# A gated mix of two attentions: the keys' first half loaded behind the first queries, and the first unit's maxima taken half by half

## The chip, the cores and the metric

The kernel runs on one core of one Trainium2 chip. The metric is the device time of one execution in microseconds; of several runs the median is given.

## The reference

Two attention blocks read the same input `x` (2048 rows, 448 columns, 16 heads of 28) and are mixed row by row by a sigmoid gate.

```python
qkv = x @ wqkv                       # for A and for B, split into q, k, v of 16 heads
# A: each position sees itself and 7 earlier ones at a distance of 2
logits = einsum("bhsd,bhswd->bhsw", q, k[idx]) * 28 ** -0.5     # idx = pos - 2 * (0..7), masked
a = (softmax(logits) applied to v[idx]) @ A_wo
# B: full attention
p = softmax(einsum("bhqd,bhkd->bhqk", q, k) * 28 ** -0.5)
b = einsum("bhqk,bhkd->bhqd", p, v) @ B_wo
g = sigmoid((x * gate_w).sum(-1, keepdims=True))
out = g * a + (1 - g) * b
```

## The kernel before

The kernel's order is written out by hand: each engine takes its instructions in the order in which the program gives them. Nearly all DMAs are issued by one queue, SP (SyncE), also in program order. An instruction that waits holds up all that stand behind it on its engine, and a DMA whose source isn't ready holds up SP.

**Projection stage** (the first 250 us or so). The loop `for n, t in enumerate(tiles)` computes one tile of the product `x @ wqkv` a turn. The tiles 0 to 27 are B's queries and keys, 128 rows of the transposed product by 512 positions, then follow B's values and A's queries, keys and values. Each float32 operand is split in a rounded part and a rest (`hi`, `lo`; `xh`/`xl`, `wh`/`wl`), so a tile takes 11 matmuls. The order of the first tiles is, as (position block `nb`, row group `k`): (0,1), (0,0), (0,2), (1,1), (1,2), (1,0), (2,1), (3,1), (2,0), (2,2), (3,0), (3,2). Row group 1 holds the keys of the first four heads, row group 0 their queries. So the keys of positions 0 to 1023 come from tiles 0 and 3, those of 1024 to 2047 from tiles 6 and 7, and the first 512 queries from tile 1.

- The tiles 0 to 9 (`n < FULL`) use the whole array. `qk_tile` (L344 to L349) takes the result out of PSUM with ScalarE (L348) and VectorE (L349), and `qk_store` sends both parts to DRAM (`qk_hi`, `qk_lo`) on SP, through `dma_r` (L99).
- From tile 10 on `project_halves` works with the two 64-row halves of the array side by side: 21 half matmuls a tile. ScalarE copies both partial sums (L353, `raw`), GpSimd adds them (L355), ScalarE rounds (L358) and GpSimd takes the rest (L359). The copy and the `hi`/`lo` pair lie in a pool of eight rotating buffers (`pp`, `pair`).

**The maxima, spread over the program.** B's softmax needs each query's maximum over all keys ahead of its exponentials. For that the scores are computed a first time with the rounded parts. A unit `u` is 512 queries of four heads; there are 16. A unit's maxima are 64 matmuls of 128 queries (`qs`) by 512 keys (`kc`) for one head (`h`), issued by `s1_mm` (L142), and VectorE reduces each result to one number per query (L148, L164) in a column of `MX`. From tile 11 on each tile of the projection carries four of these matmuls (`s1_half`), which stand behind the second and the eighth of the tile's products in each half. A unit thus spans 16 tiles. In the first unit the number `i` of a matmul within the unit gives `qs = i // 16`, `kc = i // 4 % 4`, `h = i % 4`: tile 11 reads keys 0 to 511, tile 12 keys 512 to 1023, tile 13 keys 1024 to 1535, tile 14 keys 1536 to 2047, all for the first 128 queries, and so on.

When a unit's 64 maxima are there, `max_parts` folds the four of each query and head with one reduction on VectorE (L176), and ScalarE and GpSimd turn the result into two parts, which go to DRAM (`nm`) and are read with the queries of the attention stage.

**The loads for it.** `load_qhi(u)` brings a unit's queries to `QP` (four DMAs, one for each head, L99), and `load_k` brings keys to `KH` (four DMAs as well). In the loop the first queries are loaded at `n == 3`; the keys of the first four heads come in two halves, positions 0 to 1023 at `n == 5` and 1024 to 2047 at `n == 8`. In the same turns stand, in this order: the tile's own stores, the loads of the next weights (`load_w`, at `n` 2 and 3), `load_qhi(0)` and `load_k`.

**Attention stage** (from some 255 us). For each unit and each block of 128 keys TensorE computes the scores with three products (L980), ScalarE the exponentials (L985), TensorE their product with the values (L946); the rest of the maxima (L142, L148) and all of A's windowed attention (GpSimd, VectorE) are laid beside it by a planner with estimated costs. The last stage is the output projection (L832).

Of the kernel before, what the change touches and what calls it, by code (L numbers as in the profile page):

```python
# [11 lines left out]
ALU = mybir.AluOpType  # L12
X = mybir.AxisListType.X
ET = mybir.EngineType

S, D, H, DH = 2048, 448, 16, 28
# [5 lines left out]
NMX = 192  # L22
# [3 lines left out]
def gated_mix_kernel(ctx: ExitStack, tc: tile.TileContext, xT, xn, gw, wA, wB, woAB, out):  # L26
# [4 lines left out]
    qk_hi = dram.tile([2 * D, S], F32R, name="qk_hi")  # L31
# [39 lines left out]
    KH = [cp.tile([128, S], F32R, name=f"KH{i}") for i in range(2)]  # L71
    KL = [cp.tile([128, S], F32R, name="KL0")]
    MX = cp.tile([128, NMX], F32, name="MX")
# [24 lines left out]
    def dma_r(dst, src):  # L98
        nc.sync.dma_start(dst.bitcast(F32), src.bitcast(F32))  # L99


    def load_k(g, t, src, c=slice(0, S)):
        for h in range(4):
            r = D + 112 * g + DH * h
            dma_r(t[32 * h:32 * h + DH, c], src[r:r + DH, c])
# [23 lines left out]
    def load_qhi(u):  # L129
        g, b = divmod(u, NB)  # L130
        qhis[u] = QP[u % 2]
        for h in range(4):
            r = 112 * g + DH * h
            dma_r(qhis[u][h % 2][32 * h:32 * h + DH, :], qk_hi[r:r + DH, 512 * b:512 * b + 512])

    def s1_mm(n, bank, half=False):
        u, i = divmod(n, 64)
        qs, kc, h = i // 16, i // 4 % 4, i % 4
        if i == 0 and u + 1 < NU:
            load_qhi(u + 1)  # L140
        r = slice(64 * (h // 2), 64 * (h // 2) + 64) if half else slice(32 * h, 32 * h + DH)
        nc.tensor.matmul(bank, qhis[u][h % 2][r, 128 * qs:128 * qs + 128],  # L142
                         KH[u // NB % 3][r, 512 * kc:512 * kc + 512], start=True, stop=True)
# [29 lines left out]

    def max_parts(u, later=None):
        m = sp.tile([128, 16], F32, name="m")
        nc.vector.tensor_reduce(m.rearrange("p (h q) -> p q h", h=4),  # L176
                                MX[:, 64 * u % NMX:64 * u % NMX + 64].rearrange("p (q k h) -> p q h k", q=4, h=4),
                                axis=X, op=ALU.max)
        t = sp.tile([128, 32], F32R, name="nmt")
        v = sp.tile([128, 16], F32, name="nmv")  # L180
        nc.scalar.activation(t[:, 0:16], m, AF.Copy, scale=-1.0)
        nc.scalar.activation(v, m, AF.Copy, scale=-1.0)
        low = lambda: nc.gpsimd.tensor_tensor(out=t[:, 16:32], in0=v, in1=t[:, 0:16].bitcast(F32), op=ALU.subtract)
        if later:
            later(low)
        else:
            low()
        return t
# [6 lines left out]
    def max_store(u, r):  # L195
        for a in range(4):
            nc.sync.dma_start(nm[u].bitcast(F32)[:, 32 * a:32 * a + 32], r[32 * a:32 * a + 32, :])  # L197
# [14 lines left out]
    with tc.tile_pool(name="xp", bufs=1) as xp, tc.tile_pool(name="wp", bufs=2) as wp:  # L212
# [28 lines left out]
        def split_x(nb):  # L241
            r, t = xst[:, nb, 0:3, :], xst[:, nb, 3, :]
            for kt in range(3):
                split(xh[nb][:, kt, :], xl[nb][:, kt, :], r[:, kt, :])
            tail = xh[nb][:, 3, :]
            nc.scalar.activation(tail, t, AF.Copy)
            o = LOW[nb]
            nc.vector.tensor_tensor(out=tail[o], in0=t[o], in1=tail[o].bitcast(F32), op=ALU.subtract)
# [3 lines left out]
        def load_w(wi, tails=(False, True)):  # L252
            src, cols = WSRC[wi]
            if wi not in wraw:
                wraw[wi] = raw3(), wp.tile([128, 450], F32, tag="wt", name="wt"), sum(c1 - c0 for c0, c1 in cols) + 2 * (wi == GATE)
            r, t, _ = wraw[wi]
            for tail in tails:
                o = 0
                for c0, c1 in cols:
                    e = o + c1 - c0  # L260
                    if tail:
                        both(t[:, o:e], src[384:448, c0:c1])
                    else:
                        nc.sync.dma_start(r[:, :, o:e], src[0:384, c0:c1].rearrange("(k p) c -> p k c", p=128))
                    o = e

                if wi == GATE:
                    if tail:
                        both(t[:, o:o + 2], gw[0:2, 384:448].rearrange("i p -> p i"))
                    else:  # L270
                        for kt in range(3):
                            nc.sync.dma_start(r[:, kt, o:o + 2],
                                              gw[0:2, 128 * kt:128 * kt + 128].rearrange("i p -> p i"))

        def split_w(wi, kts):
            if wi not in wsets:
                wsets[wi] = [wp.tile([128, 4, 450], F32R, tag=g, name=f"{g}{wi}") for g in ("wh", "wl")]
            wh, wl = wsets[wi]
            r, t, n = wraw[wi]
            for kt in kts:  # L280
                split(wh[:, kt, :n], wl[:, kt, :n], r[:, kt, :n] if kt < 3 else t[:, :n], nc.gpsimd)
# [24 lines left out]
        def project(n):  # L306
            order = FIRST if n == 0 else ORDER
            for i, p in enumerate(order):
                product(n, p, None, i == 0, i == len(order) - 1)
                if n == 0 and i == 0:  # L310
                    warm(3)
# [109 lines left out]
        for kt in range(3):  # L421
            if kt < 2:
                nc.vector.tensor_copy(xh[0][:, kt, :], r[:, kt, :])
            nc.vector.tensor_tensor(out=xl[0][:, kt, :], in0=r[:, kt, :], in1=xh[0][:, kt, :].bitcast(F32),
                                    op=ALU.subtract)
        nc.vector.tensor_tensor(out=tail[64:128], in0=t[64:128], in1=tail[64:128].bitcast(F32), op=ALU.subtract)
        nc.vector.tensor_tensor(out=wl0[:, 3, 0:256], in0=wt0[:, 0:256], in1=wh0[:, 3, 0:256].bitcast(F32),
                                op=ALU.subtract)
# [3 lines left out]
        def split_third():  # L432
            c = slice(256, 384)
            for kt in range(3):
                split(wh0[:, kt, c], wl0[:, kt, c], wr1[:, kt, 128:256])
            split(wh0[:, 3, c], wl0[:, 3, c], wt0[:, c])
# [19 lines left out]
        for n, t in enumerate(tiles):  # L456
            wi = t[0]
            for w in loads:
                if loads[w] == n:
                    load_w(w)  # L460
            for w in splits:
                i, k = (n - splits[w][0]) * splits[w][1], splits[w][1]
                if 0 <= i < 4:
                    split_w(w, range(i, i + k))
            if n == 0:
                split_third()
            if n in (3, 5):
                split_x((n + 1) // 2)
            if n < FULL:
                project(n)  # L470
            else:
                project_halves(n, [S1_START <= m < S1_START + 80 for m in (n, n + 1)])
            if t[1] == "qk":
                qk_tile(n, t[2], t[3])
            elif t[1] == "v":
                add_halves(n, V[:, t[2], :, 0:DH])
            else:
                a_tile(n, t[2], t[3])
            if n == 0:
                split_x(1)  # L480
            while fini and fini[0][0] <= n:
                fini.pop(0)[1]()
            if n in (2, 3):
                load_w(1, (n == 3,))
            if n == 3:
                load_qhi(0)
            if n in (5, 8):
                load_k(0, KH[0], qk_hi, slice(0, 1024) if n == 5 else slice(1024, S))
            if n == 16:
                for i in (1, 2):  # L490
                    nc.sync.dma_start(a_scr[i][:, 0:NJ, :].rearrange("c j e -> c (j e)").rearrange(
                        "c (a b) -> c a b", b=NJ), omg[0:8, None, :].to_broadcast([8, 56, NJ]))
            if n == 32:
                nc.gpsimd.memset(V[:, :, :, DH:], 1.0)
            if n == 22:
                load_k(1, KH[1], qk_hi)
            if n == 62:
                load_k(0, KL[0], qk_lo)
            if parts and parts[0][0] <= n:
                _, u, t = parts.pop(0)  # L500
                max_store(u, max_turn(t))
            if finished and n < len(tiles) - 3:
                u = finished.pop(0)
                parts.append((n + 3, u, max_parts(u)))
            if n == 64:
                gate = []
                for sgn, dst in ((-1.0, g_t), (1.0, omg)):
                    e = sp.tile([128, NJ], F32, name="ez")
                    nc.scalar.activation(e, zt, AF.Exp, scale=sgn)
                    nc.gpsimd.tensor_tensor(out=e, in0=e, in1=V[:, 0, :, DH], op=ALU.add)  # L510
                    gate.append((dst, e))
            if n in (66, 68):
                nc.vector.reciprocal(*gate.pop(0))
            if n == 70:
                nc.sync.dma_start(og_scr.rearrange("(j p) -> p j", j=NJ), omg)
            if n == 76:
                load_q(0)
# [183 lines left out]
    for c in range(8):  # L701
# [20 lines left out]
        n = 0  # L722
# [321 lines left out]
    u = NU - 1  # L1044
# [30 lines left out]
```

## Time and profile before

| | |
|---|---|
| three timed runs | 904.98, 905.28, 903.61 us; median 904.98 |
| the profiled execution | 903.91 us, of which the span is 902.1 |
| granted TensorE clock, mean | 1.0 |
| TensorE matmuls | 8326, busy 895.1 us |
| VectorE, ScalarE, GpSimd busy | 737.1, 644.3, 640.5 us |
| DMA | 105.04 MB, mean 116 GB/s |

Times of instructions are counted from the start of the span. "PE" is TensorE's matmuls, "PEld" its weight loads, which run beside the matmuls before them; "SPq" is SP's queue, whose rows give the time of issuing a DMA and not that of its transfer. A row of the timeline gives start, duration, engine, line, operation, the tile written and the tiles read, the shape and the count; in brackets stands the idle time ahead of it with what ended it. A row of the waits gives a total, a count and the longest, in us. A row of the windows gives for a stretch the busy time of PE, PEld, DVE, ACT and POOL with their instruction counts, then the granted clock, the DMA engines' busy share and GB/s.

### The profile page before, as it was taken

Reading aid. Unit: us, or ns where it says so; the run is one execution under the profiler, and the core shown is the slowest. Engines: PE = TensorE matmul, PEld = TensorE weight load, DVE = VectorE, ACT = ScalarE, POOL = GpSimd, SP = SyncE. Lnnn points to the kernel's source line nnn. Section 1 sums busy time; section 2 is a strip of 40 time slices with the busy share of each in tenths; the row PEclk is TensorE's granted clock in tenths of the full one; section 3 lists DMA queues with packets and bytes.
Section 4 is the critical chain, followed back from the end, with each engine's and each line's share of the span. In section 5 each row is a group of like instructions: output and inputs, shape, how many; then the busy total and the mean of one; then the engine's idle time right before and its main releaser. Section 6 shows DMA issues by size and latency. Waiting matters only on the chain. (4 is left out here: it accounts for less than half of the span.)

```text
span 902.1 us, 20546 instructions
## 1 busy us (share of the span) xinstructions
PE 895.1 (99%) x8326; PEld 539.3 (60%) x8326; DVE 737.1 (82%) x961; ACT 644.3 (71%) x770; POOL 640.5 (71%) x507
## 2 busy tenths in 40 slices
PE   9999999999999999999999999999999999999998
PEld 7799999999954444444444444444444444434997
DVE  6588999998979999999999999999999999821221
ACT  6456434343378888988988989889888898898220
POOL 2389847464459689999999998999999699501000
PEclk9999999999999999999999999999999999999999
DMA  9877503449373241226225242352220222245791
GB/s 265 286 254 195 161 12 84 134 127 112 105 252 78 92 128 52 69 51 163 71 53 144 86 114 57 94 140 62 55 65 19 89 43 57 75 95 164 211 280 65
DMA packets 116758, 105.04 MB, mean 116 GB/s; under 512 B 77192, under 2 KB 84744, under 8 KB 115880
## 3 DMA queue, kind: packets, MB, share of 16 engines
q1 hardware_dynamic: 116520, 103.47, 41.9%
q8 instruction: 65, 1.06, 0.5%
q10 hardware_dynamic: 144, 0.26, 0.1%
q14 instruction: 29, 0.24, 0.1%
HBM read 62.72 MB, written 40.96 MB: 115 GB/s over the span
## 5 line engine op out<-in xcount | busy, mean ns | idle before, releaser
L985 ACT ACTIVATE P<-T 128x1024 f32<-128x1024 f32 x512 | 496.8, 1024 | 60.4 <-PE T L980 58.3
L148 DVE TENSOR_REDUCE MX<-T 128x1 f32<-128x512 f32 x470 | 442.1, 954 | 34.2 <-PE T L142 17.8
L946 PE MATMUL av<-P,V 128*32 128x512 f32 x2048 | 272.7, 605 | 0.4 <-ACT osb L850 0.4
L980 PEld LDWEIGHTS T<-QH,KH 30*128 30x128 f32 x1024 | 92.5, 181 | 231.1 <-ACT P L985 197.3
L142 PE MATMUL T<-KH,QP 28*128 28x512 f32 x704 | 219.9, 455 | 0.1
L980 PE MATMUL T<-QH,KH 30*128 30x512 f32 x1024 | 212.5, 489 | 0.6 <-DMA QH<-nm 0.4
L164 DVE TENSOR_REDUCE MX<-r 128x2 f32<-128x1024 f32 x160 | 192.2, 1222 | 25.5 <-PE r L142 21.7
L980 PE MATMUL T<-QH,KL 28*128 28x512 f32 x1024 | 187.0, 395 | 0.0
L980 PE MATMUL T<-QL,KH 28*128 28x512 f32 x1024 | 184.7, 392 | 0.0
L609 POOL TENSOR_TENSOR prod<-qt,kt 128x896 f32<-128x896 f32 x64 | 135.5, 2117 | 5.1 <-DMA kt<-a_scr 5.0
L367 ACT ACTIVATE raw<-r 128x896 f32<-128x896 f32 (+1 forms) x64 | 58.9, 921 | 98.0 <-PE r L304 93.3
L670 POOL TENSOR_TENSOR oat<-oat,prod 128x896 f32<-128x896 f32 x48 | 101.2, 2108 | 2.0
L142 PEld LDWEIGHTS T<-KH,QP 28*128 28x128 f32 x704 | 86.0, 181 | 27.4 <-ACT P L985 20.3
L368 POOL TENSOR_TENSOR ast<-raw 128x448 f32<-128x448 f32 x48 | 55.3, 1153 | 59.0 <-ACT raw L367 48.5
L665 POOL TENSOR_TENSOR prod<-vt,L 128x896 f32<-128x896 f32 x56 | 95.3, 1702 | 0.2
L980 PEld LDWEIGHTS T<-QL,KH 28*128 28x128 f32 x1024 | 94.4, 184 | 0.0
L980 PEld LDWEIGHTS T<-QH,KL 28*128 28x128 f32 x1024 | 93.4, 183 | 0.4
L946 PEld LDWEIGHTS av<-P,V 128*32 128x32 f32 x2048 | 40.3, 108 | 77.8 <-issue 65.3
L304 PE MATMUL r<-wh,xh 64*128 64x448 f32 (+1 forms) x512 | 82.9, 363 | 0.0
L142 PE MATMUL r<-KH,QP 64*128 64x512 f32 x320 | 80.6, 394 | 0.6 <-DMA KH<-qk_hi 0.4
L304 PE MATMUL r<-wh,xl 64*128 64x448 f32 (+1 forms) x384 | 70.4, 364 | 0.0
L614 POOL TENSOR_TENSOR prod<-prod 128x448 f32<-128x448 f32 x64 | 65.5, 1024 | 5.0
(112 smaller groups left out, 1076.7 us busy)
## 6 DMA issues: line engine op xcount, KB each, us to landing
a_scr<-ast SPq DMA_DIRECT2D x24, 448.0 KB
qk_hi<-qkh SPq DMA_DIRECT2D x24, 256.0 KB
qk_lo<-qkh SPq DMA_DIRECT2D x24, 256.0 KB
rbc<-rs SPq DMA_DIRECT2D x64, 64.0 KB
QP<-qk_hi SPq DMA_DIRECT2D x64, 56.0 KB
KL<-qk_lo SPq DMA_DIRECT2D x16, 224.0 KB
QH<-qk_hi SPq DMA_DIRECT2D x64, 56.0 KB
QL<-qk_lo SPq DMA_DIRECT2D x64, 56.0 KB
```

The lines of the kernel that those rows point to most:

```text
L142: nc.tensor.matmul(bank, qhis[u][h % 2][r, 128 * qs:128 * qs + 128], KH[u // NB % 3][r, 512 * kc:512 * kc + 512], start=True, stop=True)
L148: i = nc.vector.tensor_reduce(MX[:, n % NMX:n % NMX + k], bank, axis=X, op=ALU.max)
L164: nc.vector.tensor_reduce(m, PM[k], axis=X, op=ALU.max)
L304: nc.tensor.matmul(bank[:, 0:cols], x, ws[c][rows, k, 0:cols], start=first, stop=last)
L367: nc.scalar.activation(raw[:, :, 0:cols], PJ[n % 2][:, :, 0:cols], AF.Copy)
L609: nc.gpsimd.tensor_tensor(out=p, in0=qt[c], in1=kvt["k", c % 2][:, HALO - DIL * w:HALO - DIL * w + NJ, :], op=ALU.mult)
L614: nc.gpsimd.tensor_tensor(out=lo, in0=lo, in1=hi, op=ALU.add)
L665: nc.gpsimd.tensor_tensor(out=dst.rearrange("p j (h d) -> p j h d", d=DH), in0=kvt["v", c % 2][:, HALO - DIL * w:HALO - DIL * w + NJ, :].r ...
L670: nc.gpsimd.tensor_tensor(out=ows[c % 2][:, :, 0:56] if w == W - 1 else oat[c], in0=oat[c], in1=oat[c, w], op=ALU.add)
L946: nc.tensor.matmul(av[32 * h:32 * h + 32, :], V[:, kt, 4 * g + h, :], tiles_[h], start=(kt == 0), stop=(kt == NJ - 1), skip_group_check=True)
L980: nc.tensor.matmul(bank[a], (KH[g % 3], KH[g % 3], KL[g % 2])[t][r, ks], (qh, ql, qh)[t][r, :], start=(t == 0), stop=(t == 2))
L985: e = nc.scalar.activation(p, one if a == "2" else mine, AF.Exp, scale=SCALE).ins
```

## The change

Three places. The keys' first half is loaded at `n == 3`, behind the first queries, and not at `n == 5`. In the first unit (`u == 0`) the order of the 64 matmuls is another: the tiles 11 to 18 take the keys 0 to 1023 for all 512 queries, the tiles 19 to 26 the keys 1024 to 2047. The columns of `MX` then hold the first unit's maxima in the order (key half, query block, key block within the half, head), so its fold reduces over two inner axes (the key half and the key block) in one instruction. The other units are as before.

```diff
     def s1_mm(n, bank, half=False):
         u, i = divmod(n, 64)
         qs, kc, h = i // 16, i // 4 % 4, i % 4
+        if u == 0:
+            qs, kc = i // 8 % 4, 2 * (i // 32) + i // 4 % 2
         if i == 0 and u + 1 < NU:
             load_qhi(u + 1)
...
     def max_parts(u, later=None):
         m = sp.tile([128, 16], F32, name="m")
+        mx = MX[:, 64 * u % NMX:64 * u % NMX + 64]
         nc.vector.tensor_reduce(m.rearrange("p (h q) -> p q h", h=4),
-                                MX[:, 64 * u % NMX:64 * u % NMX + 64].rearrange("p (q k h) -> p q h k", q=4, h=4),
-                                axis=X, op=ALU.max)
+                                mx.rearrange("p (q k h) -> p q h k", q=4, h=4) if u else
+                                mx.rearrange("p (a q k h) -> p q h a k", a=2, q=4, h=4),
+                                axis=X if u else mybir.AxisListType.XY, op=ALU.max)
...
             if n == 3:
                 load_qhi(0)
-            if n in (5, 8):
-                load_k(0, KH[0], qk_hi, slice(0, 1024) if n == 5 else slice(1024, S))
+            if n in (3, 8):
+                load_k(0, KH[0], qk_hi, slice(0, 1024) if n == 3 else slice(1024, S))
```

## The prediction

> **What bounds the kernel now.** The page comes first, for the size of things.
>
> ```profile
> span 902.1 us, 20546 instructions
> PE 895.1 (99%) x8326; PEld 539.3 (60%) x8326; DVE 737.1 (82%) x961; ACT 644.3 (71%) x770; POOL 640.5 (71%) x507
> ```
>
> TensorE has work almost without a break, so a change counts if it takes idle time from TensorE or adds some. The edit touches the projection stage (about the first 250 us) and there the keys' first loads, so I next asked for the waits of the first 60 us, and kept the rows of L142, the maxima's matmuls, which are the first readers of the keys.
>
> ```profile
> PEld r L142 <- issue: 1.2, 2, 0.6
> PEld r L142 <- DMA KH<-qk_hi: 0.5, 1, 0.5
> PE r L142 <- DMA KH<-qk_hi: 0.4, 2, 0.2
> ```
>
> The same stall has two sizes. The matmul row (PE) shows 0.4 us, the weight-load row (PEld) 1.2 + 0.5 = 1.7 us. Which is right is decided by the timeline of the weight loads, since TensorE takes its instructions in order and a held weight load holds all behind it:
>
> ```profile
> 35.51 0.20 PEld L299 LDWEIGHTS r<-xh,wh 64*128 64x128 f32 x2
> 36.27 0.18 PEld L142 LDWEIGHTS r<-KH,QP 64*128 64x128 f32 x1 [0.56 <-issue]
> 36.30 0.26 PEld L299 LDWEIGHTS r<-xh,wh 64*128 64x128 f32 x2
> 37.09 0.18 PEld L142 LDWEIGHTS r<-KH,QP 64*128 64x128 f32 x1 [0.53 <-DMA KH<-qk_hi]
> ...
> 42.10 0.60 PEld L299 LDWEIGHTS r<-xh,wh 64*128 64x128 f32 x3
> 43.35 0.31 PEld L142 LDWEIGHTS r<-KH,QP 64*128 64x128 f32 x2 [0.65 <-issue]
> ...
> 46.15 0.29 PEld L142 LDWEIGHTS r<-KH,QP 64*128 64x128 f32 x2
> ...
> 57.75 0.28 PEld L142 LDWEIGHTS r<-KH,QP 64*128 64x128 f32 x2
> 36.30 0.47 PE L142 MATMUL r<-KH,QP 64*128 64x512 f32 x1 [0.16 <-DMA KH<-qk_hi]
> 43.38 0.59 PE L142 MATMUL r<-KH,QP 64*128 64x512 f32 x2 [0.24 <-DMA KH<-qk_hi]
> ```
>
> Three holes: 0.56 us (tile 11, heads 0 and 1), 0.53 (tile 11, heads 2 and 3) and 0.65 (tile 13). Two are marked "issue" on the weight-load side, but the matmul rows of the same instants name the key load. The code agrees: tile 11 is the first to read keys 0 to 511, and tile 13 the first to read keys 1024 to 1535, which are the second load. Together 1.74 us. A count by itself: from 46.15 to 57.75 four tiles pass, 2.90 us each. Three tiles before 46.15 tile 11's first maxima matmul would stand at 37.45 in that rhythm; it could have gone at 35.71 (35.51 + 0.20). The difference is 1.74 us again, so the time is lost to TensorE and not made up.
>
> [...] By the matmul rows the sum below would be 0.4 us, by the weight loads 1.7; the 2.90 us rhythm speaks for the second.
>
> **The keys' first load, moved.** All of these DMAs are issued by one queue, SP. Its timeline around the change (each line is issue time, not transfer):
>
> ```profile
> 22.62 0.34 SPq L99 DMA_DIRECT2D qk_hi<-qkh  x1
> 23.29 0.34 SPq L99 DMA_DIRECT2D qk_lo<-qkh  x1
> 24.21 3.25 SPq L226 DMA_DIRECT2D wt<-in_wB  x4
> 27.50 1.85 SPq L99 DMA_DIRECT2D QP<-qk_hi  x4
> 29.45 0.35 SPq L99 DMA_DIRECT2D qk_hi<-qkh  x1
> ...
> 30.85 0.40 SPq L99 DMA_DIRECT2D qk_lo<-qkh  x1
> 31.35 2.09 SPq L99 DMA_DIRECT2D KH<-qk_hi  x4
> 33.53 0.34 SPq L99 DMA_DIRECT2D qk_hi<-qkh  x1
> ...
> 34.44 0.49 SPq L99 DMA_DIRECT2D qk_hi<-qkh  x1
> ...
> 38.84 1.60 SPq L99 DMA_DIRECT2D KH<-qk_hi  x4
> ...
> 40.97 0.37 SPq L99 DMA_DIRECT2D qk_lo<-qkh  x1
> 41.38 2.13 SPq L99 DMA_DIRECT2D QP<-qk_hi  x4
> ```
>
> The four key DMAs leave 31.35 and go behind the queries' four, which end at 29.35. They pass the four stores of tiles 4 and 5 (29.45 to 31.25) and so come 31.35 - 29.4 = 1.95 us earlier. What they read was written by tiles 0 and 3; tile 3's stores were issued at 22.62 and 23.29. How long a store takes until its reader may go can be read once: tile 7's was issued at 34.44 and the second key load passed SP at 38.84, 4.4 us. Tile 3's pair is then through by 27.7 (23.29 + 4.4), before 29.35, so the new place adds no wait on SP; the margin is 1.6 us. Behind the moved load stand the stores of tiles 4 and 5, now about 2.1 us later, at 31.5 to 33.4. Their reader is the second queries' load at 41.38, 8 us off. From tile 6 (33.53) on the queue stands as before.
>
> Landing: the first pair of heads was released 36.27 - 31.35 = 4.9 us after the load's start, the second 37.09 - 31.35 = 5.7. From 29.4 that is 34.3 and 35.1. TensorE wants them at 35.71 and about 35.9 (one 0.18 us weight load later). Margins 1.4 and 0.8 us, so both holes go: 0.56 + 0.53 = 1.09 us. I take the whole; if the load lands 0.8 us later than reckoned it begins to cost again, and at most the old 1.09 stays.
>
> **The order of the first unit.** The keys' second half is now first read in tile 19 instead of tile 13. At 2.90 us a tile that is 17.4 us later, against a release at 43.35: the third hole, 0.65 us, goes whatever the first load does. The number of matmuls, their shapes and the number of maxima are unchanged (64 of L142 in the unit in either order), so no other term comes from it.
>
> **The fold.** One reduction in place of one reduction, over the same 64 values per partition, with two inner axes instead of one:
>
> ```profile
> L176 DVE TENSOR_REDUCE m<-MX x16: 254/267/275, 84.6 to 785.1; 128x16 f32<-128x64 f32 x16
> 80.00:100.00 20.00, 20.00 (x188) 20.00 (x186) 17.75 (x18) 9.85 (x16) 19.15 (x18) 1.00 0.81 237
> ```
>
> No row shows a reduction over two axes. Below, it could gain a few tens of ns (254 is the fastest of its kind); above, I bound it by the 1.2 us of the 1024-value reductions of the next fence. It is done once, and VectorE has 20 - 17.75 = 2.25 us to spare in those 20 us, so I take 0.0 on the path; without that cover it would be at most 1 us, once.
>
> **What is late next.** After the stalls go, TensorE runs tiles 13 onward 1.7 us earlier, and its followers must come along:
>
> ```profile
> 42.25 1.22 DVE L164 TENSOR_REDUCE MX<-r 128x2 f32<-128x1024 f32 x1 [0.40 <-PE r L299]
> 46.21 1.02 ACT L353 ACTIVATE raw<-r 128x1024 f32<-128x1024 f32 x1 [1.94 <-PE r L299]
> 49.13 1.03 ACT L353 ACTIVATE raw<-r 128x1024 f32<-128x1024 f32 x1 [1.38 <-PE r L299]
> 64.72 1.29 POOL L355 TENSOR_TENSOR raw<-raw 128x512 f32<-128x512 f32 x1 [0.33 <-ACT raw L353]
> 400.00:500.00 100.00, 100.00 (x1027) 41.69 (x1022) 94.24 (x136) 88.86 (x102) 96.57 (x68) 1.00 0.41 107
> PE av L946 <- ACT osb L850: 0.4, 1, 0.4
> PE T L980 <- DMA QH<-nm: 0.4, 1, 0.4
> ```
>
> VectorE, ScalarE and GpSimd wait here for TensorE or for each other, so they move with it. In the whole run TensorE's longest other waits (last two rows) are 0.4 us, and the transfer in them is fed by TensorE's own maxima. Nothing later is tied to absolute time, the program's order is fixed, and the attention stage keeps TensorE busy for 100.00 of 100 us. I take the gain as kept to the end.
>
> **Sum.** 0.56 + 0.53 + 0.65 = 1.74, say 1.7 us less. The profiled execution took 903.91 us: 902.1 of span and 1.8 around it; with the change 902.2. It lies 1.07 under the median of the three timed runs (904.98; 903.61 to 905.28). The four executions have the mean 904.45, and 904.45 - 1.74 = 902.7 is my time. A change of 0.2% is 1.8 us (about what a measurement of this kernel can tell from no change); the mark is 903.17. The forecast lies 0.5 under it, with about that much uncertainty in a median of three.
>
> **Rivals.**
> 1. *The load still lands late.* Its bytes meet other traffic, or the two "issue" holes are not the keys'. Then only the attributed 0.53, or only the third hole's 0.65, goes: 903.8 to 903.9. For it: the margin for heads 2 and 3 is 0.8 us, and the DMA engines are 92% busy in the 20 us that hold the moved load:
>
> ```profile
> 20.00:40.00 20.00, 19.73 (x110) 15.69 (x110) 9.78 (x15) 9.13 (x18) 5.15 (x5) 1.00 0.92 308
> ```
>
>   Against it: the matmul rows name the keys at two of the holes. The lower end of this is the matmul rows' 0.4 us, 904.05.
> 2. *Slower through SP and a buffer.* Tiles 10 onward copy both partial sums into one of eight rotating pair buffers; tile 13's copy is the 21st use, tile 9's halves the 13th, so tile 13's copy must wait for tile 9's last store (issued 40.97). Wanted now at 46.21 - 1.7 = 44.5; with 4.4 us to land the store frees it at 45.4, 0.9 late, and the copy ends at 46.4. TensorE needs the bank for tile 15 at 49.13 - 1.7 = 47.4, so 1.0 us is left. If SP is held at the moved load by tile 3's stores for d, tile 9's store is late by as much, and TensorE loses d - 1.0. It ends slower from d = 2.7, and by over 0.2% from d = 4.5; at d = 5 the sum is 904.45 - 1.74 + 4.0 = 906.7. Against it: that needs tile 3's stores to take over 10 us where 4.4 was seen.
> 3. *Another rhythm in the attention stage.* The weight loads there idle by 197.3 us for the exponentials:
>
> ```profile
> PEld T L980 <- ACT P L985: 197.3, 236, 1.1
> ```
>
> If GpSimd's and VectorE's side work falls a little otherwise, 1% of this is 2 us, either way: 900.7 or 904.7. All engines move together, so I give it little.
> 4. *Nothing.* The second key load or another engine takes over each hole: 904.45.
>
> **How the numbers follow.** Forecast 0.70 (0.49 beyond the mark, 0.21 short of it, by the half microsecond above). Rival 1 has 0.11 (0.02 faster, 0.09 same), rival 2 0.07 (slower), rival 3 0.09 (0.04, 0.02, 0.03), rival 4 0.03 (same). Sums: faster 0.55, same 0.35, slower 0.10. The range reaches from 901.4 (the fastest timed run 903.61 less 1.74, and 0.5 below) to 905.0 (rival 4 with 0.5 on top).
>
> **What would show it.** Right: in the profile after, the SP timeline has the four KH DMAs directly behind the four QP ones near 29.4 and the stores of tiles 4 and 5 behind them; the weight loads of L142 have no hole near 35.7, 36.5 and 42; tile 14's pair, 46.15 here, stands near 44.4; the first stretch of the attention stage begins 1.7 us earlier; and the span is near 900.4. Wrong: a hole left on KH in tile 11, an SP wait ahead of the moved load, a new wait for the exponentials' buffers that grows over the attention stage, or a two-axis fold much over 0.3 us with ScalarE waiting behind it.

## The result

| | before | changed |
|---|---|---|
| median of 10 runs each | 904.05 us (903.32 to 905.28) | 901.91 us (901.58 to 903.16) |
| profiled execution | 903.91 us, span 902.1 | 902.23 us, span 900.5 |

The ratio is 0.9978, with a 95% interval of 0.9970 to 0.9986: 2.1 us faster. The forecast was 902.7 us (901.4 to 905.0), faster by 1.74 us. That range also held a kernel with no gain at all (904.45 us), so the time alone says little about the mechanism; the rows below do.

The profile page of the changed kernel, its size lines. The matmul count and the busy time of the side engines are what they were:

```profile
span 900.5 us, 20546 instructions
PE 893.1 (99%) x8326; PEld 527.6 (59%) x8326; DVE 737.6 (82%) x961; ACT 644.1 (72%) x770; POOL 640.5 (71%) x507
```

The weight loads are busy for 12 us less with the same count (527.6 against 539.3). That is no gain: from 48 to 86 us, behind the three holes, their busy time falls from 38.0 to 32.8 us, while TensorE's matmuls fill all 38 us before and after. Why the loads take less there is open.

The timeline of the weight loads at the same place (start, duration, then as before; L142 is L144 now and L299 is L303). The first row is the start of tile 10, the switch to half arrays:

```profile
33.79 0.76 PEld L303 LDWEIGHTS r<-xh,wh 64*128 64x128 f32 x8 [0.36 <-issue]
...
36.20 0.20 PEld L303 LDWEIGHTS r<-xh,wh 64*128 64x128 f32 x2
36.44 0.18 PEld L144 LDWEIGHTS r<-KH,QP 64*128 64x128 f32 x1
36.45 0.41 PEld L303 LDWEIGHTS r<-xh,wh 64*128 64x128 f32 x2
36.68 0.18 PEld L144 LDWEIGHTS r<-KH,QP 64*128 64x128 f32 x1
...
42.26 0.40 PEld L144 LDWEIGHTS r<-KH,QP 64*128 64x128 f32 x2
```

No bracket stands behind any of the L144 rows: the three holes are gone. Tile 11's first maxima start within 0.24 us of the loads before them, and tile 13's pair at 42.26 goes without a wait.

SP's timeline (issue times) shows how:

```profile
28.53 1.85 SPq L99 DMA_DIRECT2D QP<-qk_hi  x4
30.48 1.61 SPq L99 DMA_DIRECT2D KH<-qk_hi  x4
32.19 0.35 SPq L99 DMA_DIRECT2D qk_hi<-qkh  x1
...
33.60 0.72 SPq L99 DMA_DIRECT2D qk_lo<-qkh  x1
...
39.53 1.61 SPq L99 DMA_DIRECT2D KH<-qk_hi  x4
```

The keys' four DMAs stand 0.1 us behind the queries' four, with no wait between, and the stores of tiles 4 and 5 (32.19 to 34.3) behind them. The queue as a whole was about 1 us later in this execution than in the first profile (28.53 against 27.50); that is chance and not the change, as it lies ahead of the edit.

**Where the time came from.** The spans differ by 1.6 us, but the two executions already differ ahead of the edit: tile 10 starts at 33.79 instead of 33.09, and these 0.7 us are there at TensorE's last wait for a part of the input (16.50 against 15.80 us). A measure free of that is the length of the stage from tile 10's first weight load to the first matmul of tile 28 (the first product of the values). Before, it went from the first of these rows to the second, 86.50 - 33.09 = 53.41 us:

```profile
33.09 0.76 PEld L299 LDWEIGHTS r<-xh,wh 64*128 64x128 f32 x8 [0.36 <-issue]
...
86.50 0.68 PE L304 MATMUL r<-wh,xh 64*128 64x448 f32 x4
```

Now it ends here:

```profile
85.39 0.37 PE L308 MATMUL r<-wh,xh 64*128 64x448 f32 x1
```

85.39 - 33.79 = 51.60 us. The edit took 1.81 us out of this stage in this pair of profiles. The experiments use the same measure.

### The profile page after: what moved, and what is told of

It reads as the page before. It is cut to its first block, busy times and chain, and to the rows that moved or that the text cites. A ratio compares the mean times of both kernels' runs of the same rounds, so it can differ in the third digit from the quotient of the medians.

```text
span 900.5 us, 20546 instructions
## 1 busy us (share of the span) xinstructions
PE 893.1 (99%) x8326; PEld 527.6 (59%) x8326; DVE 737.6 (82%) x961; ACT 644.1 (72%) x770; POOL 640.5 (71%) x507
## 3 DMA queue, kind: packets, MB, share of 16 engines
q1 hardware_dynamic: 116520, 103.47, 42.2%
## 4 chain that ended last, share of the span: by engine, by line
PE 97%; DMA 1%; ACT 1%; DVE 0%; SPq 0%; issue 0%; ACTq 0%
PE T L984 31%; PE av L950 28%; PE r L308 15%; PE T L836 8%; PE r L303 7%; PE r L144 4%; PE T L144 4%; DMA V<-in_xT 1%; ACT P L989 1%; DVE MX L166 0%; SPq L230 0%; ACT raw L371 0%; PE av L1034 0%; DVE xh L252 0%; ACT xh L250 0%
## 5 line engine op out<-in xcount | busy, mean ns | idle before, releaser
L989 ACT ACTIVATE P<-T 128x1024 f32<-128x1024 f32 x512 | 496.7, 1024 | 60.0 <-PE T L984 58.7
L950 PE MATMUL av<-P,V 128*32 128x512 f32 x2048 | 272.7, 605 | 0.4 <-ACT osb L854 0.4
L144 PE MATMUL T<-KH,QP 28*128 28x512 f32 x704 | 220.2, 456 | 0.1
L144 PE MATMUL r<-KH,QP 64*128 64x512 f32 x320 | 105.2, 392 | 0.3 <-DVE MX L166 0.3
L144 PEld LDWEIGHTS T<-KH,QP 28*128 28x128 f32 x704 | 86.0, 181 | 27.5 <-ACT P L989 18.6
L308 PE MATMUL r<-wh,xh 64*128 64x448 f32 (+1 forms) x512 | 93.2, 363 | 0.0
L950 PEld LDWEIGHTS av<-P,V 128*32 128x32 f32 x2048 | 40.3, 108 | 78.1 <-issue 65.3
L308 PEld LDWEIGHTS r<-wh,xh 64*128 64x128 f32 x512 | 74.1, 185 | 2.5
L308 PE MATMUL r<-wh,xl 64*128 64x448 f32 (+1 forms) x384 | 73.5, 364 | 0.0
```

The lines of the kernel that those rows point to most:

```text
L308: nc.tensor.matmul(bank[:, 0:cols], x, ws[c][rows, k, 0:cols], start=first, stop=last)
L950: nc.tensor.matmul(av[32 * h:32 * h + 32, :], V[:, kt, 4 * g + h, :], tiles_[h], start=(kt == 0), stop=(kt == NJ - 1), skip_group_check=True)
L989: e = nc.scalar.activation(p, one if a == "2" else mine, AF.Exp, scale=SCALE).ins
```

## The experiments

Of each kernel I give the holes in its weight loads on the keys, the length of the stage just defined, and the ratio to the kernel before on the same chip.

**1. The early load alone** (`load_only`, twice): the kernel before with only

```diff
-            if n in (5, 8):
-                load_k(0, KH[0], qk_hi, slice(0, 1024) if n == 5 else slice(1024, S))
+            if n in (3, 8):
+                load_k(0, KH[0], qk_hi, slice(0, 1024) if n == 3 else slice(1024, S))
```

> The early load alone; the first unit keeps its old order (tile 13 reads keys 1024 to 1535) and its old fold. Theory (every hole that the keys tear into TensorE's weight loads is lost time, and is kept to the end): the two holes of tile 11 (0.56 and 0.53 us) are gone, the one of tile 13 (0.65 us) stays or grows a little, since TensorE now arrives there 1.1 us earlier and the second load lands when it did: between 0 and 1.1 us less than before, nearest to 0, because the tile 13 hole should grow from 0.65 to about 1.7. Rival (the holes are separate terms that add up): 1.0 us less than before, ratio 0.9989. Second rival (the measured gain of 2.1 us comes mostly from elsewhere, later in the program): 1.5 to 2.1 us less.

> The early load with the old order, once more. Theory: no hole in tile 11, one in tile 13 that is as large as all three of before together (1.7 us in the first profile; 1.7 to 2.5 here); low clocks in some of the executions, since the hole is in one piece; the others are within 0.5 us of before. Rival: the tile 13 hole stays near 0.65, about 1 us less than before; low clocks as rare as in the kernel before.

Measured: ratio 0.9995 (0.9984 to 1.0005), and 1.0003 (0.9993 to 1.0013) the second time: no gain over all executions. The weight loads of the first profile, then the weight-load and the matmul row of the second:

```profile
36.12 0.18 PEld L142 LDWEIGHTS r<-KH,QP 64*128 64x128 f32 x1
36.36 0.18 PEld L142 LDWEIGHTS r<-KH,QP 64*128 64x128 f32 x1
...
43.82 0.31 PEld L142 LDWEIGHTS r<-KH,QP 64*128 64x128 f32 x2 [1.72 <-DVE MX L164]
```

```profile
44.57 0.31 PEld L142 LDWEIGHTS r<-KH,QP 64*128 64x128 f32 x2 [2.56 <-issue]
...
44.60 0.59 PE L142 MATMUL r<-KH,QP 64*128 64x512 f32 x2 [2.15 <-DMA KH<-qk_hi]
```

Tile 11 runs without a hole and TensorE then stands at tile 13 until the second half of the keys is there: one hole of 1.72 us (marked with VectorE, whose last reduction had ended at 42.88 us, 0.94 us before; the matmul row of the second profile names the keys), and 2.56 us of weight loads in the second profile. The three holes of before sum to 1.74 in its first profile. So the early load by itself only moves the wait. The theory's "nearest to 0" holds for the profiles: the stage took 53.51 and 54.35 us, against 53.88 in the mean of three profiles of before. The first interval still takes in the rival's 0.9989; the second does not, and a hole that grew from 0.65 to 1.72 and 2.56 us speaks against holes that simply add up.

One expectation missed. Nine of the 22 executions had a mean granted clock of 0.998 or less (the last section comes back to them). The other 13 were expected within 0.5 us of before, but in the means they lie 0.8 and 0.95 us under it (904.03 against 904.85, then 904.04 against 905.00, low clocks left out on both sides). That is close to the rival's 1.0. A reading that fits is that the clock fell in the executions with the longest holes, which leaves the shorter ones here; no run shows it, and this part stays open.

**2. The new order alone** (`order_only`, twice): the change with the first load back in its old place,

```diff
-            if n in (3, 8):
-                load_k(0, KH[0], qk_hi, slice(0, 1024) if n == 3 else slice(1024, S))
+            if n in (5, 8):
+                load_k(0, KH[0], qk_hi, slice(0, 1024) if n == 5 else slice(1024, S))
```

> The new order of the first unit and its fold; the keys' first half is loaded at n == 5 as before. Theory: the holes of tile 11 stay (1.09 us), the one of tile 13 goes (0.65 us): 0.6 us less than before, ratio 0.9993, TensorE 0.6 us ahead from tile 14 on. Rival (the order is worth nothing by itself, a second wait takes the place): 0.0. Second rival (gain elsewhere): over 1.2 us less.

> The new order with the old place of the first load, once more. Its first profile had one hole of 1.63 us and one of 0.75, and 3.4 us of half clock behind them. Theory (the clock is halved in some executions by a long enough hole; the executions without that show the holes alone): this profile, if its clock stays at 1.00, has holes in tile 11 of 1.1 to 2.4 us and none in tile 13; executions with a mean clock of 0.998 or less are 1.5 to 3 us above the others; the others lie 0.2 to 0.6 us under those of before. Rival (the half clock is a chance of that one execution and has nothing to do with the holes): low clocks are as rare here as in the kernel before (2 of 43).

Measured: ratio 1.0005 (0.9995 to 1.0015), then 0.9994 (0.9983 to 1.0005). The first interval leaves out the expected 0.9993; the second takes it in, and takes in no gain as well. Both profiles have their holes in tile 11 only, so the order does what was expected of it. The first profile (906.79 us):

```profile
37.65 0.18 PEld L144 LDWEIGHTS r<-KH,QP 64*128 64x128 f32 x1 [1.63 <-issue]
...
38.69 0.18 PEld L144 LDWEIGHTS r<-KH,QP 64*128 64x128 f32 x1 [0.75 <-DMA KH<-qk_hi]
...
40.06 0.33 PEld L144 LDWEIGHTS r<-KH,QP 64*128 64x128 f32 x1
```

The holes here are 2.38 us, and then the weight loads themselves take 0.33 us instead of 0.18. The windows around it (the third number from the end is the granted clock):

```profile
33.00:39.60 6.60, 5.04 (x37) 3.43 (x37) 1.07 (x2) 1.62 (x2) 2.17 (x3) 0.98 0.98 300
39.60:43.00 3.40, 3.40 (x20) 3.21 (x18) 1.92 (x2) 0.00 (x0) 0.00 (x0) 0.53 0.71 258
43.00:50.00 7.00, 7.00 (x64) 6.85 (x62) 5.41 (x6) 4.19 (x6) 5.10 (x4) 1.00 0.79 249
```

For about 3.4 us the clock is half (0.53 in the second window), with 20 matmuls where the 2.90 us rhythm of 25 a tile gives 29. The stage took 55.17 us, 3.57 over the 51.60 without holes. In the second profile, without half clock, it took 52.32, with these holes:

```profile
36.16 0.18 PEld L144 LDWEIGHTS r<-KH,QP 64*128 64x128 f32 x1 [0.72 <-DMA KH<-qk_hi]
...
36.79 0.18 PEld L144 LDWEIGHTS r<-KH,QP 64*128 64x128 f32 x1 [0.33 <-issue]
```

That is 1.05 us, just under the 1.1 to 2.4 expected. Of the second time's 12 executions, two had a clock of 0.997; they took 907.1 us in the mean, 2.9 over the other ten (904.2), as expected. The ten lie 0.8 us under those of before on the same chip (905.0), a little more than the 0.2 to 0.6 expected. Two low clocks of 12, against 2 of 23 of before there, don't settle by themselves whether the holes cause them.

**3. The load later still** (`late7`): the change with the first load behind tile 7's stores,

```diff
-            if n in (3, 8):
-                load_k(0, KH[0], qk_hi, slice(0, 1024) if n == 3 else slice(1024, S))
+            if n in (7, 8):
+                load_k(0, KH[0], qk_hi, slice(0, 1024) if n == 7 else slice(1024, S))
```

> The change, but the keys' first half is loaded at n == 7, behind tile 7's stores, where SP stands near 35.5 us. With 4.9 and 5.7 us from issue to release as in the profile before, the first matmul of the maxima is held until 40.4, the third of the same tile until 41.2: a hole of about 5.5 us where before there were 1.74 in all. Theory (lost time of TensorE in this stage reaches the end undiminished): 5.5 - 1.74 = 3.8 us more than before, ratio 1.0042. Rival (later stages have slack that gives early shifts back): less than half of it, under 1.9 us more.

Measured: 908.09 us against 904.87, ratio 1.0040 (1.0024 to 1.0056). The interval leaves the rival out. But the agreement with 1.0042 is partly luck. In the profiled execution the holes are 5.3 us (the first is marked with a store, but the matmul row of the same instant names the keys' load, KH<-qk_hi, with 4.37 us):

```profile
42.90 0.28 PEld L144 LDWEIGHTS r<-KH,QP 64*128 64x128 f32 x1 [4.78 <-DMA qk_hi<-qkh]
...
43.92 0.28 PEld L144 LDWEIGHTS r<-KH,QP 64*128 64x128 f32 x1 [0.52 <-issue]
```

Its stage took 59.10 us, 7.5 over 51.60: 5.3 us of holes, and about 2.2 us since the clock was half behind them (0.54 granted from 42 to 44 us, 0.58 from 44 to 50). This was the longest of its seven executions, 912.44 us, and in it tile 10 began at 35.51 us, 1.7 us or more later than in every other profile. I can't split the other six.

That later stages give nothing back can be read directly. From tile 28's first matmul to the end of the span this execution took 816.0 us (910.6 - 94.61). The three profiles of before took 815.2 to 815.9 us for it, the four without holes 815.1 to 816.7. A stage that is 7.5 us longer leaves the rest as it was, within the scatter of these executions.

**4. The change and the kernel before, profiled again** (`change_again`, `before_again`, `before_third`; no edit).

> The changed kernel once more, for a second profile and for the size on the same chip as the others. Theory: 1.6 to 1.7 us of the gain arise between 33 and 46 us of the span; the shares seen at 214 us (0.24) and at 796 us (0.45) and the 0.7 us lost before 17 us in the first pair of profiles are chance and come out otherwise here. Rival: they belong to the change and come back with the same sign and size. Either way about 1.7 to 2.1 us less than before, ratio 0.9977 to 0.9981.

> The kernel before, profiled a second time. Theory (the size of the holes differs between executions, since the SP queue's moment differs, and the first profile was of an execution with small ones: 903.91 us against a median of 904.9): holes on the keys of 1.7 us or more, up to about 3, and a time that is higher by about as much as the holes exceed 1.7. Rival (the holes are the same 1.74 us in each execution and the rest of the gain lies elsewhere): 1.7 us again, whatever the time.

> The kernel before, profiled a third time, for the same question: theory, holes between 1.7 and 3 us that move with the time; rival, 1.74 us again.

The change again: 902.66 us against 904.87, ratio 0.9974 (0.9964 to 0.9984), no hole, stage 51.60. The two single executions of before took 904.58 and 904.46 us. Their holes, first one kernel, then the other:

```profile
36.87 0.18 PEld L142 LDWEIGHTS r<-KH,QP 64*128 64x128 f32 x1 [0.94 <-DMA KH<-qk_hi]
37.91 0.18 PEld L142 LDWEIGHTS r<-KH,QP 64*128 64x128 f32 x1 [0.74 <-DMA KH<-qk_hi]
...
44.41 0.31 PEld L142 LDWEIGHTS r<-KH,QP 64*128 64x128 f32 x2 [0.88 <-DVE MX L164]
```

```profile
36.12 0.18 PEld L142 LDWEIGHTS r<-KH,QP 64*128 64x128 f32 x1 [0.69 <-DMA KH<-qk_hi]
...
36.77 0.18 PEld L142 LDWEIGHTS r<-KH,QP 64*128 64x128 f32 x1 [0.35 <-issue]
...
43.65 0.31 PEld L142 LDWEIGHTS r<-KH,QP 64*128 64x128 f32 x2 [1.27 <-DVE MX L164]
```

2.56 and 2.31 us, where the first profile had 1.74. The times are 0.67 and 0.55 us over that profile's 903.91, for holes that are 0.82 and 0.57 us longer: the theory holds, and the rival (1.74 us each time) is out. The queue's moment explains part of it: the second key load was issued 5.75, 6.55 and 5.83 us after tile 10's start (33.09, 33.32, 32.82 us), and released tile 13 some 4.5, 4.5 and 5.0 us later. All profiles without half clock together (the first of the order alone, 55.17 us, and the late load, 59.10 us, stand above):

| kernel | holes on the keys, us | stage, us | over 51.60 |
|---|---|---|---|
| before, three profiles | 1.74, 2.56, 2.31 | 53.41, 54.25, 53.97 | 1.81, 2.65, 2.37 |
| early load alone, two | 1.72, 2.56 | 53.51, 54.35 | 1.91, 2.75 |
| order alone, second profile | 1.05 | 52.32 | 0.72 |
| the change, two; and experiments 5 and 6 | 0 | 51.60, 51.60; 51.60, 51.61 | 0 |

The four executions without holes agree within 0.01 us, and a stage is longer by about what its holes are long. In the three profiles of before the stage is 2.28 us longer in the mean. That is the gain: 2.1 us in the first comparison, 2.2 in the second.

The other differences that the first two profiles show come out otherwise in the later ones, and so are taken as chance. The 0.7 us ahead of tile 10 are 0.25 in the change's second profile (33.34 against 33.09). The attention stage's last wait for queries,

```profile
PEld T L980 <- DMA QH<-nm: 1.3, 1, 1.3
```

is in the first profile of before alone of the three, and appears in the second of the order alone (0.95 us) and in those of experiments 5 and 6 too (0.84 and 1.01 us).

**5. A little later than the change** (`step4`): the first load at `n == 4`, behind tile 4's stores.

```diff
-            if n in (3, 8):
-                load_k(0, KH[0], qk_hi, slice(0, 1024) if n == 3 else slice(1024, S))
+            if n in (4, 8):
+                load_k(0, KH[0], qk_hi, slice(0, 1024) if n == 4 else slice(1024, S))
```

> The change, but the keys' first half is loaded at n == 4, one tile's stores (about 1.0 us of SP) later than in the change. With 4.9 and 5.7 us from issue to release and an issue near 31.4 in the profile after, the halves' wants at 36.44 and 36.68 are met at 36.3 and 37.1. Theory (time of the load's landing against the moment of want is all that counts): a hole of 0 to 0.5 us, so 0 to 0.5 us more than the change, 1.7 to 2.3 us less than before, ratio 0.9975 to 0.9981. Rival (what helps is that the load passes the stores of both tiles): half of the gain gone, ratio 0.9988.

Measured: 902.48 us against 904.77, ratio 0.9972 (0.9961 to 0.9983). The gain is whole, so passing both tiles' stores isn't needed: the rival is out. In the profile the load's issue begins 2.86 us after the queries' (1.95 in the change), and there is no hole:

```profile
27.32 1.85 SPq L99 DMA_DIRECT2D QP<-qk_hi  x4
...
30.18 1.69 SPq L99 DMA_DIRECT2D KH<-qk_hi  x4
...
```

```profile
35.68 0.18 PEld L144 LDWEIGHTS r<-KH,QP 64*128 64x128 f32 x1
35.92 0.18 PEld L144 LDWEIGHTS r<-KH,QP 64*128 64x128 f32 x1
```

The second pair of heads was wanted 5.74 us after the load's start (35.92 - 30.18) and was there. In the profile of the change it was wanted 6.20 us after (36.68 - 30.48). If the load took no longer there, the change has a margin of 0.46 us or more; the longest such time on record is 5.90 us (38.69 - 32.79, the first profile of the order alone).

**6. The second half late** (`second14`): the change with

```diff
-            if n in (3, 8):
+            if n in (3, 14):
```

> The change, and the keys' second half is loaded at n == 14 instead of n == 8. In the new order tile 19 is its first reader, some 14 us after the new place. Theory (off the path): the same time as the change, ratio to before 0.9974 to 0.9978; SP's wait ahead of the second load (1.2 us in the profile after) goes, which nobody waited for. Rival (the second load's place still matters, through SP): over 0.5 us more or less than the change.

Measured: 902.75 us against 904.77, ratio 0.9979 (0.9969 to 0.9989), stage 51.61. The ratio lies just over the expected 0.9974 to 0.9978, and its interval alone wouldn't exclude the rival's half microsecond; the stage does. The second load, six tiles later, is off this stage's path, as expected, and SP's wait ahead of it (1.1 us in the change, 38.4 to 39.53 us) is gone without effect.

Neither of the two variants with a whole gain is shown to be better than the change.

## Why the prediction was right, point by point

- **Weight loads over matmul rows.** The matmul rows put 0.4 us on the keys, the weight loads 1.7. The stage lost 1.81, so the second is right here. The larger holes show how the two differ: where the matmul row shows a hole at full clock, it is 0.40 to 0.41 us shorter than in the weight-load row (1.23 for 1.63, 2.15 for 2.56), so a small hole nearly vanishes there (0.16 for 0.56). The busy share of the weight loads (60% before, 59% after) would have shown nothing here; it was the idle time ahead of single loads that told.
- **Place on SP.** Right in each part: the load directly behind the queries' (30.48 behind 28.53 + 1.85), no wait ahead of it, tiles 4 and 5 behind it, and nothing that waited for their stores. The time of its landing can't be read where nobody waits; experiment 5 suggests that it is some 0.5 us or more earlier than needed (0.8 was forecast).
- **The third hole goes by the order.** Right, shown by the order alone, with no hole in tile 13. What I did not say is that the holes aren't separate terms: while tile 13's stays, removing the two of tile 11 doesn't shorten the stage, as tile 13's grows by as much (experiment 1). The sum was right only because the change makes both edits.
- **Fold.** Right. In VectorE's timeline of the changed kernel it takes what the others of its line take (0.255 to 0.275 us, median 0.268):

```profile
83.83 0.27 DVE L179 TENSOR_REDUCE m<-MX 128x16 f32<-128x64 f32 x1
```

- **Kept to the end.** Right: 2.28 us in the stage's mean, 2.1 and 2.2 in the times. TensorE's first product with the values (L946, now L950) starts at 258.55, 259.70 and 259.64 us in the profiles of before, and at 257.40, 257.26, 257.22 and 257.88 in the four without holes, 1.9 us earlier in the mean. That the span of 900.5 was forecast as 900.4 is partly luck: 1.81 us came off the stage, 0.7 were lost ahead of it and 0.5 came off behind it by chance. And one reading here broke the prediction's own rule: it took TensorE's longest other wait from the matmul rows, as 0.4 us, where the weight-load row of the same wait (QH<-nm, above) has 1.3. It did no harm, as that wait comes and goes with and without the change. The rhythm of the attention stage is what it was, which speaks against the third rival:

```profile
PEld T L984 <- ACT P L989: 197.3, 236, 1.1
```

- **The buffer behind SP (second rival).** No sign of it; the copies of the half tiles wait for TensorE alone (17 times, 21.2 us together in the changed kernel).
- **The term that was mis-sized.** 1.74 us was read from one execution. Three have a mean of 2.20 us of holes (2.28 in the stage), and the first was the smallest. The base was too high as well: 904.45 us from four executions, 904.05 in ten. Both errors, 0.4 us each, make the time too high: 902.7 was forecast, 901.91 measured.
- **Not foreseen.** That the clock was half for some 3.4 us behind holes of 1.63 and 0.75 us (below), and that kernels with holes had a tail of long executions with a low clock (906.2 us in the mean against 904.0 with the early load alone). The mean part of this in the change's gain is small: of the 66 executions of before that were measured beside the experiments, 4 had a mean granted clock of 0.998 or less.

## What to carry to other kernels

When TensorE waits for several loads in a row, removing the first wait can simply make the next one longer (here from 0.65 to 1.72 and 2.56 us): ask for the last of them, and edit the order of reading together with the place of loading. Measure a wait for a DMA in more than one execution before it goes into a sum, since it goes with when the queue gets to the DMA (the second key load here 5.75 to 6.55 us after tile 10's start) and how long that takes (4.5 to 5.0 us), and here lay between 1.7 and 2.6 us. And measure a stage between two of its own landmarks: 51.60 us four times over told more than times that differ by a microsecond from run to run.

## What the runs showed of the hardware

In two of the profiles the holes in TensorE's work cost more than themselves: the late load's (4.78 and 0.52 us; the stage was 7.5 us longer) and the first of the order alone (1.63 and 0.75 us; the stage was 3.57 us longer). The early load's hole of 2.56 us was not followed by a lower clock (1.00 from 43 to 50 us), so the length of the hole doesn't decide it alone. In the order alone, first profile, the matmul rows stood idle for only 1.23 and 0.34 us:

```profile
37.68 0.47 PE L144 MATMUL r<-KH,QP 64*128 64x512 f32 x1 [1.23 <-DMA KH<-qk_hi]
...
38.72 0.47 PE L144 MATMUL r<-KH,QP 64*128 64x512 f32 x1 [0.34 <-DMA KH<-qk_hi]
```

and the clock was then half for some 3.4 us (0.53 granted from 39.6 to 43 us). Stretches of 0.2 us put this spell from 39.4 to 42.8 us, and that of the late load from 42.2 to 49.0 us, 6.8 us (0.57 granted from 43 to 50 us). Executions with a mean granted clock of 0.998 or less: none of 34 of the three kernels without holes (the change, experiments 5 and 6), 4 of 66 of before (holes of 1.7 to 2.6 us in three pieces), 5 of 23 of the order alone (1.05 to 2.4 us in two pieces), 9 of 22 of the early load alone (1.7 to 2.6 us in one piece), 7 of 7 of the late load (5.3 us). The holes are those of the profiles; the other executions' weren't measured. The 9 of the early load took 906.2 us in the mean, the other 13 took 904.0. That the single piece is what matters is a reading of these counts and wasn't tried by itself.

When the clock of the late load fell at 42.2 us, TensorE had stood idle for 3.6 us (its matmul at 42.93 has 4.37 us of idle time ahead of it). In the order alone the idle time ahead of the spell was shorter, 1.57 us in the matmul rows and 2.38 in the weight loads. Why only some executions have such a spell is not shown by any run here.
